# Broadcast rows, V copies and inverse deviations moved to other engines in a fused adaLN, sliding-window attention and token-mixer kernel

## The chip, the core and the metric

The kernel runs on one core of a Trainium2 chip. The core has five engines with instruction streams of their own: TensorE (PE, matrix products, with its weight loads listed as PEld), VectorE (DVE), ScalarE (ACT), GpSimd (POOL) and SyncE (SP, which here only issues DMAs). The metric is the device time of one execution in microseconds (us).

## The reference

One sequence of 2048 tokens (`S`), width 512 (`D`), 32 heads of 16. All inputs are bf16.

```python
mod = (silu(c) @ w_mod).reshape(1, 6, 1, 512)          # c: (1, 512), w_mod: (512, 3072)
sa, ca, ga, sb, cb, gb = mod[:, 0], ..., mod[:, 5]

h = layernorm(x) * (1 + ca) + sa
q, k, v = split(h @ wqkv)                              # 32 heads of 16
p = softmax(mask(q @ k.T * 16**-0.5))                  # key j for query i: 0 <= i - j < 256
x = x + ga * ((p @ v) @ wo)

h = layernorm(x) * (1 + cb) + sb
n = layernorm(h)
u = gelu(n.T @ w1 + b1)                                # over tokens: w1 is (2048, 1792)
y = (u @ w2 + b2).T                                    # w2 is (1792, 2048)
x = x + gb * y
```

## The kernel before

**Groups and chunks.** Tokens are worked on in four groups `G` of 512 (four tiles of 128 rows). Each group has a normalisation (`l1st` statistics, `l1rs` the inverse deviation, `l1nm` the negated mean, `xn` the normalised tile), transposes (`tr`), the modulation while the transposes are evicted (`h1T`), the products `q`, `k`, `v`, then attention, and then `post`: the output product (`wo`), the residual (`x2`), two more normalisations (`l2`, `l3`) and the modulation `c2`, `s2` between them, which give `hb`. Attention runs in eight units `u` of 256 queries, cut into 75 chunks. Chunk `i` is a score product `S{i}` into four PSUM banks (tiles `psa`, three banks, one buffer, and `psb`, one bank, two buffers), two exponentials on ACT (`E{i}` over three banks, `F{i}` over the fourth, both into `et`), for chunks 35 to 74 masks on DVE (`M{i}`; the earlier chunks add the mask inside PE), and the product `AV{i}` with V and with ones into `pxy`. When a unit's four heads' block is done, ACT takes `ln` and `rz` (tile `lz`, the reciprocal of the sum) and DVE multiplies (`OT`).

After attention come the products of the token mixer. `p` and `p2` are the parts over token groups that are ready early (tile `pu`, added up in `part`), `m1` the rest, `m2m` the second layer; `f1`, `f2` finish the output tiles.

**Order.** Nothing is scheduled at run time. Every piece of work is an `op` with a number, and the string `ORDER` (lines 45 to 99) lists all 1388 of them; `run_order` emits them in that order, and a letter behind a number (A, D, P) sets the engine where there is a choice of ACT, DVE or POOL. So each engine has a fixed instruction order, and an engine whose next instruction has to wait holds up everything behind it. All instructions from `ORDER` show in the profile under line L194, that of the wrapper which emits them, so they are told apart by tile names.

**PSUM.** Almost all products other than scores share two banks, `psd`, in turn (tiles `pq`, `pv`, `pt`, `pa`, `pu`, `ps_b`). PE can start the next of them when the one two earlier has been evicted.

**What the change touches.**

- *First shift.* For the first 256 tokens Q and K are made from `h1p`, which has the scale `1 + ca` alone, and the shift `sa` reaches them as a bias `qkb` from a product of `wqkv` with `sa2` (`e_b`, `e_bc2`, op `qkb`). V uses `h1T`, with scale and shift. Both kernels have this.
- *Modulation rows* `ga`, `1+cb`, `sb`, `gb`, wanted in all 128 partitions: `bc` makes the four rows in one PSUM bank, each in its own 32 partitions (four products at a time in different columns of the array, weights `sT_rep` of 32 columns), `bce` evicts them with a factor and an addend per partition, `bcw` writes 4 KB to a DRAM scratch and `bcl` reads that back to all partitions as `bc_all`.
- *Inverse deviation* (`e_rs`): on ACT as Ln and then Exp (x -0.5), or on POOL as an addition and a power. `ORDER` sends the nine of groups 1 to 3 (first norm) and 0 to 2 (second and third norm) to POOL.
- *V* (`v(tb)`, 16 tiles of tokens): the product leaves PSUM in a layout of two halves, one for each parity of heads, and each parity goes to its own 64 partitions of `VT`, with zeros in the other 64. For group 0 two copies `ve` of 64 partitions (8 in all) write into a `VT` that was zeroed before (`vz`). For groups 1 to 3 one copy `vn` of 128 partitions goes to SBUF, and two POOL multiplications `vp` by 1 or 0 (`half_m`) write both halves of `VT`, data and zeros.

Of the kernel before, what the change touches and what calls it, by code (L numbers as in the profile page):

```python
# [45 lines left out]
43 3 0 4 41 2 36 1 48 7 52 8 40 5 87 56 34 80P 6 46 9 57 37 10 58 84 39 11 33 12 88 35 13 50 14 59 89 31 90D 15 60  # L46
16 54 61 51 95D 17 65 96D 18 63 66 19 104 20 64 99 108A 47 21 67 53 100A 22 68 91 102A 23 24 105A 118 55 25 45 107A
101D 26 92 106A 119 27 115 103A 42 28 121 32 116 83P 120 49 62 69 117D 141 70 142 81D 133 143A 134 323 146 135A 147
38 136 148A 130 324 131 145 44 132A 149 137 150 325 138 151A 139 93 194 94D 140A 326 126 97P 195 122 144 123 82P 127
196 198 128D 327P 129A 98D 199 124D 153 71 125D 152 328D 200 109 72 73 206 110A 111D 207 112 74 197 114D 113D 201  # L50
180 181 202 154 182D 155 203 214 184 208 204 161 85 29 156D 215 162 788 30 205 209 164D 177 210 178 216 163D 222 211
165 223 212 183 166 179D 157 168D 158 167A 213 159D 217 224 160D 188 218 76 229 79 219 172 230 189 220 173 77 221
225 190D 174D 191 169 226 548 170 231 176 233 175 227 171D 185 234 186 192 228 193 329D 232 330D 331D 237 235 332D
333 187D 238 334 337 336D 338 236 335D 339D 245 239 340D 344 246 549 354 345 78 249 247 346D 355 250 348 240 356D
364 365 241 256 366D 251 388 257 789 349 389 242 260 258 243 350 261 244 351D 248 252 390D 264 253 550 391 262 372
265 75 358 373 86 369 374D 370 254 272 371D 266 341 273 551 380 381 255 342 382D 274 276 343D 384 259 277 263 347
359 267 357 278 394 360 395 352 286 361D 375 287 268 288 398 367 396 283 790 399 376 284 385 285 552P 386 269 402
400 270 791 363 271 403 275 368 279 387D 295 280 362 411 404 377 281 353 289 412 282 378 392 397 379D 393 553P 415
413 554P 296 401 416 383 405 290 555D 292 406 556D 422 417 291 557P 293 407 423 558 408 410 559 294 409 414 560D 424
427 297 418 428 561D 562 563 605 565D 419 431 564D 429 298 606 432 584 300D 299P 585 607D 420 586D 439 433 613 421  # L60
440 594 301D 595 302P 444 441 426 425 303D 792P 445 614 430 615D 451 446 596D 617 434 452 569 304P 570 443 435 305D
455 1033 453 571D 306P 1032 597 456 602 598 616 436 460 307P 457 437 603 313 461 308P 438 442 599D 447 604D 462 468
309P 448 589 469 590 579 310P 591D 449 472 588 470 450 580 314 473 459 454 572 458 311D 593 581D 480 474 566 793D
481 609 567 608 463 568D 464 484 315 601 482 574 485 592 610 575 600 465 488 486 582 466 576D 489 467 471 587 475
583 476 497 477 573 611 490 478 618 1031 612D 498 483 487 794D 312D 491 795P 316 492 501 499 508 479 796P 502 509
511 317P 512 493 619 503 494 797P 318D 620 495 510 500 320P 504 520 321P 505 625 513 621 517 506 319D 624 514 626
322P 507 515 622 496 577 521 630 627 578 518 516 631 519 623 628 639 632 522 798 640 802 799 803 523 633 644 641
524P 629 645 804D 634 525D 800D 526P 635 801D 652 646 805D 806 653 642 807 527D 809 808D 810 528P 636 657 654 811D
814 658 637 819 529D 815 647 530D 662 659 816D 638 663 643 660 648 531D 538 842 649 671 664 655 843 650 532D 672 820
651 533P 656 821D 665 676 673 661 677 534P 844D 853 539 666 667 535P 684 678 540 854 685 850 818 855D 851 536D 837  # L70
668 852D 537P 686 689 669 838 690 834 839D 835 674 694 691 679 670 687 695 675 692 680 836D 829 681 541 703 696 845
682 846 542P 704 683 830 697 688 543D 708 705 831D 546P 693 709 824 547D 812 698 847D 825 699 544D 716 710 545P 826D
1038 717 1039 706 1043 822 1040 700 721 711 718 1041 857 701 722 1044 1042D 840 702 707 813 726 723 1049 856 727 712
841 1045 713 735 832 728 1046 736 1050 827 1047D 1048 1051 858 1035 724 1052 714 817 740 1053D 737 751 741 719 752
848 715 748 720 729 742 859 823 725 753 860 730 743 1054 849 749 731 864 861 833 750 1055 865 1056 760 828 1060 1061
738 732 869 866 733 1057 761 870 734 1059 739 1058D 1034 744 1037 871 878 1062 745 872 879 1065 1066 867 1063 746
883 1064D 880 1067 747 884 1068 881 757 1070 1069D 758 1036 862 891 885 759 754 892 755 863 756 868 893 762 873 896
874 1071 897 763 1072 1073 894 764P 1076 886 875 898 901 876 1074 765D 902 766P 1077 1075D 877 767D 910 903 899 882
911 768D 887 769D 1078 770D 1082 888 771D 912 778 915 1083 916 1084 904 1085 1079 772D 889 917 923 1081 890 924 895
918 1080D 900 905 773D 913 906 928 1087 907 925 1088 908 774D 929 909 926 914 775P 779 919 920 933 776D 930 1086D  # L80
1089 777P 934 1090 780 1093 1094 1091D 921 942 781 935 987 943 1095 922 782P 1096 936 927 944 931 947 988 948 1097D
932 783D 989 937 786P 990 938 999 949 785P 955 991 939 787P 956 1098 992 1099 784P 940 1100 1001 1101 1000 957 960
1103 1102D 1115 961 950 1116 1007 1118 945 1119 1002 1008 965 1117 962 941 946 966 1009 951 1120 1121 963 952 1104
1010 967 974 1011 953 1105 968 975 1122 1106 958 1107 954 1123 976 979 959 980 977 964 1108D 969 1124 1012 970 1109
1019 971 1125 981 972 1110 1020 982 973 1126 978 983 1021 993 984 1157 1171 1027 1111 985 1166 1112 1022 1092 986
1163 994 1028 1113A 1158 995 996 1159 997 1170 1003 1161 1127 1162 1128 998 1160 1004 1176 1114 1129 1130 1165 1131
1013 1167 1005 1133 1164 1188 1169 1014 1180 1006 1168 1132 1134 1015 1136 1135 1137 1016 1172 1138 1139 1200 1017
1023 1140 1184 1018 1142 1024 1025 1143 1141 1026 1029 1145 1030 1146 1144 1173 1177 1174 1189 1192 1175 1178 1204
1147 1179 1181 1185 1182 1201 1205 1186 1148 1187 1190 1193 1149 1183 1208 1191 1212 1194 1209 1150 1195 1196 1197
1151 1198 1152 1220 1199 1153 1221 1202 1154 1216 1203 1206 1155 1213 1156 1248 1210 1238 1239 1214 1258 1224 1215  # L90
1240 1207 1217 1228 1211 1218 1229 1259 1222 1241 1268 1230 1225 1260 1226 1231 1249 1227 1232 1223 1242 1278 1219
1298 1261 1233 1243 1288 1262 1250 1279 1251 1299 1252 1289 1253 1300 1254 1280 1234 1244 1235 1301 1281 1245 1282
1290 1255 1263 1246 1318 1308 1236 1283 1269 1237 1284 1270 1309 1291 1319 1310 1292 1311 1302 1271 1320 1321 1272
1264 1328 1265 1303 1273 1256 1274 1322 1275 1338 1312 1285 1329 1266 1348 1293 1267 1323 1257 1349 1247 1330 1331
1332 1324 1294 1339 1276 1340 1358 1295 1277 1333 1304 1296 1313 1286 1297 1359 1360 1305 1287 1314 1361 1315 1368
1350 1325 1334 1362 1316 1351 1326 1363 1341 1306 1342 1352 1335 1307 1369 1317 1343 1327 1344 1370 1345 1353 1378
1336 1354 1346 1371 1379 1355 1347 1364 1337 1372 1356 1373 1365 1357 1374 1380 1375 1381 1382 1376 1383 1366 1384
1385 1367 1377 1386 1387
# [55 lines left out]
def kernel(  # L154
# [62 lines left out]
    half_t = const.tile([P, 4], F32, name="half_t")  # L217
    nc.vector.memset(half_t[:], -0.5)
    ident_v = identity[:].rearrange("p (a two d) -> p a two d", two=2, d=DH)
    half_m = const.tile([P, 2], F32, name="half_m")  # L220
    nc.vector.memset(half_m[:], 0.0)
    nc.vector.memset(half_m[0:KB, 0:1], 1.0)
    nc.vector.memset(half_m[KB:P, 1:2], 1.0)
    mask_par = const.tile([P, 2], F32, name="mask_par")
    modFM = const.tile([P, 8], F32, name="modFM")
    bc_all = const.tile([P, ND * D], BF, name="bc_all")
    bc_ga, bc_cb1, bc_sb, bc_gb = (bc_all[:, n * D : (n + 1) * D] for n in range(ND))
    b1FM = const.tile([P, NF], F32, name="b1FM")
    b2FM = const.tile([P, NT], F32, name="b2FM")
    wod = const.tile([P, ND, D], BF, name="wod")  # L230

    maskt = const.tile([P, 4, KB], BF, name="maskt")
# [158 lines left out]
    bcs = modw.tile([P, D], BF, name="bcs")  # L391
    bc_m = const.tile([P, 2], F32, name="bc_m")
    nc.vector.memset(bc_m[:, 0:1], 1.0)
    nc.vector.memset(bc_m[:, 1:2], 0.0)
    nc.vector.memset(bc_m[0:32, 0:1], ZSCALE)
    nc.vector.memset(bc_m[32:64, 1:2], 1.0)

# [865 lines left out]
```

## Time and profile before

| | |
|---|---|
| median of 3 runs | 266.56 us (266.38 to 267.31) |
| the profiled execution, its own time | 266.56 us |
| its span in the profile | 264.8 us |
| PE busy | 248.2 us (94%) |
| DVE busy | 193.5 us (73%) |
| ACT busy | 185.4 us (70%) |
| POOL busy | 95.9 us (36%) |
| DMA | 25.35 MB, mean 96 GB/s |
| granted PE clock | 1.00 throughout |

Times in the profile count from the start of the span. A busy share is taken over the whole span, and the kernel has stages with different limits: loading and the first chunks, attention from the first `E0` at 17.38 us to the last `F74` at 185.9 us, and a tail of matrix products after it. Rows of a timeline give the start, the duration and the number of instructions; durations of neighbours on ACT and DVE overlap a little, so the distance from start to start (the pitch) is what one instruction takes from its engine.

### The profile page before, as it was taken

Reading aid. Unit: us, or ns where it says so; the run is one execution under the profiler, and the core shown is the slowest. Engines: PE = TensorE matmul, PEld = TensorE weight load, DVE = VectorE, ACT = ScalarE, POOL = GpSimd, SP = SyncE. Lnnn points to the kernel's source line nnn. Section 1 sums busy time; section 2 is a strip of 40 time slices with the busy share of each in tenths; the row PEclk is TensorE's granted clock in tenths of the full one; section 3 lists DMA queues with packets and bytes.
Section 4 is the critical chain, followed back from the end, with each engine's and each line's share of the span. In section 5 each row is a group of like instructions: output and inputs, shape, how many; then the busy total and the mean of one; then the engine's idle time right before and its main releaser. Section 6 shows DMA issues by size and latency. Waiting matters only on the chain.

```text
span 264.8 us, 10695 instructions
## 1 busy us (share of the span) xinstructions
PE 248.2 (94%) x4769; PEld 136.8 (52%) x4769; DVE 193.5 (73%) x435; ACT 185.4 (70%) x268; POOL 95.9 (36%) x182
## 2 busy tenths in 40 slices
PE   7898999999998988899999999999999999999993
PEld 2576667656556654455544454445444444444441
DVE  5778896777847359999948888999998730415875
ACT  3479999999999899999999999999416431000000
POOL 8755321495289945553893031440000000000000
PEclk9999999999999999999999999999999999999999
DMA  7995400000017000000014862020499800001122
GB/s 212 369 382 197 42 5 6 2 5 2 2 49 196 5 4 5 2 2 2 5 38 128 227 172 85 2 61 23 152 362 397 360 2 0 21 0 63 59 99 79
DMA packets 31599, 25.35 MB, mean 96 GB/s; under 512 B 6076, under 2 KB 29632, under 8 KB 31552
## 3 DMA queue, kind: packets, MB, share of 16 engines
q1 hardware_dynamic: 31544, 24.66, 29.5%
q8 instruction: 37, 0.61, 0.9%
q14 instruction: 10, 0.08, 0.1%
q10 hardware_dynamic: 8, 0.00, 0.0%
HBM read 22.55 MB, written 2.10 MB: 93 GB/s over the span
## 4 chain that ended last, share of the span: by engine, by line
PE 67%; ACT 19%; DVE 8%; issue 4%; POOL 0%; ACTq 0%; POOLq 0%
PE pu L194 32%; ACT et L194 15%; PE pxy L194 13%; PE psa L194 8%; PE pq L194 5%; PE pa L194 4%; PE pv L194 3%; ACT lz L194 3%; DVE st L194 2%; DVE VT L194 1%; PE pt L194 1%; DVE part L194 1%; DVE OT L194 1%; PE psb L194 1%; DVE h L194 1%
## 5 line engine op out<-in xcount | busy, mean ns | idle before, releaser
L194 ACT ACTIVATE et<-psa 128x1536 bf16<-128x1536 f32 x75 | 109.1, 1455 | 4.0 <-PE psa L194 2.1
L194 PE MATMUL pu<-hb,w1p 128*128 128x512 bf16 x224 | 53.1, 380 | 0.8 <-DVE part L194 0.8
L194 PE MATMUL pu<-guT,w 128*128 128x512 bf16 x224 | 49.0, 379 | 0.0
L194 ACT ACTIVATE et<-psb 128x512 bf16<-128x512 f32 x75 | 45.1, 601 | 0.0
L194 PE MATMUL pxy<-et,ones_bd 128*32 128x192 bf16 (+3 forms) x960 | 38.7, 233 | 0.9 <-issue 0.9
L194 PE MATMUL pxy<-et,VT 128*32 128x192 bf16 (+3 forms) x960 | 38.4, 234 | 0.9 <-DVE OT L194 0.5
L194 PEld LDWEIGHTS <-w 128*128 128x128 bf16 x224 | 21.9, 98 | 26.4
L194 PE MATMUL psa<-QT,KT 32*128 32x192 bf16 (+3 forms) x720 | 29.8, 230 | 5.6 <-ACT et L194 4.9
L194 PEld LDWEIGHTS <-w1p 128*128 128x128 bf16 x224 | 20.3, 98 | 25.5 <-issue 2.3
L194 POOL TENSOR_SCALAR KT<-kb,mask_par 128x512 bf16<-128x512 bf16 (+1 forms) x36 | 22.9, 645 | 25.9 <-DVE kb L194 22.2
L194 PE MATMUL pq<-h1T,wqkv 128*128 128x512 bf16 (+1 forms) x128 | 30.1, 355 | 0.3 <-ACT VT L194 0.3
L194 PEld LDWEIGHTS <-KT 32*128 32x128 bf16 x960 | 16.1, 92 | 26.2 <-issue 23.9
L194 PEld LDWEIGHTS <-VT 128*32 128x32 bf16 x960 | 23.6, 96 | 11.6 <-issue 10.1
L194 PE MATMUL psb<-QT,KT 32*128 32x192 bf16 (+3 forms) x240 | 29.3, 231 | 0.0
L194 DVE SCALAR_TENSOR_TENSOR o<-pu,b2FM,bc_all 128x512 f32<-128x512 f32 x16 | 11.6, 748 | 20.2 <-PE pu L194 20.0
L194 DVE TENSOR_TENSOR et<-et,maskt 128x512 bf16<-128x512 bf16 (+2 forms) x56 | 24.9, 480 | 0.6 <-ACT et L194 0.5
L194 PEld LDWEIGHTS <-ones_bd 128*32 128x32 bf16 x960 | 23.2, 97 | 1.2 <-issue 1.1
L194 DVE BATCH_NORM_STATS2 st<-x 128x6 f32<-128x512 bf16 x32 | 21.7, 680 | 1.3 <-DMA x<-in_A_x_dram 1.1
L194 DVE TENSOR_TENSOR OT<-pxy,lz 128x256 bf16<-128x256 f32 x32 | 13.4, 420 | 10.6 <-ACT lz L194 10.1
L194 PEld LDWEIGHTS <-wqkv 128*128 128x128 bf16 x192 | 14.0, 97 | 13.4 <-issue 4.8
L194 PE MATMUL pv<-wqkv,h1T 128*32 128x256 bf16 x512 | 17.9, 274 | 0.2 <-DVE VT L194 0.2
L194 PE MATMUL pa<-wod,OT 128*128 128x512 bf16 x64 | 17.3, 381 | 0.3 <-ACT part L194 0.3
(113 smaller groups left out, 358.2 us busy)
## 6 DMA issues: line engine op xcount, KB each, us to landing
w1p<-in_B_w_dram SPq DMA_DIRECT2D x14, 512.0 KB, 6.1
w<-in_B_w_dram SPq DMA_DIRECT2D x14, 512.0 KB, 8.4
wmod<-in_w_mod_dram SPq DMA_DIRECT2D x6, 512.0 KB, 5.5
x<-in_A_x_dram SPq DMA_DIRECT2D x16, 128.0 KB, 4.8
out_dram<-otile SPq DMA_DIRECT2D x16, 128.0 KB, 1.7
wqkv<-in_A_wqkv_dram SPq DMA_DIRECT2D x2, 384.0 KB, 5.4
wqkv<-in_A_wqkv_dram SPq DMA_DIRECT2D x1, 512.0 KB, 5.0
wod<-in_A_wo_dram SPq DMA_DIRECT2D x1, 512.0 KB, 8.4
```

The costliest lines, as they stand in the source:

```text
L194: ins = call(*args, **kwargs)
```

## The change

It replaces four things and the order.

1. The four modulation rows are made as full products: `sT_rep` gets 128 columns, and each of `bc2`, `bc5`, `bc4`, `bc3` is four matrix products of 128x128 by 512 in a `psd` bank of its own, evicted by DVE (`bce`) into its own tile. The scratch, the two DMAs, `bc_m` and its four memsets go.
2. `e_rs` has ACT's form alone; the nine POOL ones become Ln and Exp on ACT.
3. All 16 tiles of V leave PSUM as two copies `ve` of 64 partitions; `vn`, `vp`, `half_m` and its memsets go, and all three `VT` buffers are zeroed (12 `vz` in place of 4).
4. `ORDER` is a new list. Read off it, in each engine's order:
   - SP: the same loads in the same order up to `x15`; then `b1`, `b2` without `bcw`, `bcl`.
   - PE: `S0` stands directly behind the Q and K products of heads' block 0 (before: behind those of all four blocks); `S1` behind Q and K of blocks 1 and 3 and one V tile (before: two V tiles); `S2` behind those of block 2 and the second V tile. `bc2` stands between `S7` and `S8`, `bc5` between `S8` and `S9`, `bc4` between `S15` and `S16`, `bc3` between `S17` and `S18` (before: `bc` between `S1` and `S2`).
   - ACT: one `h1p` in place of four, one `ke` in place of three, two `qe` in place of three; the others go to DVE. The nine added Ln and Exp pairs stand after `E5`, `E18`, `E19`, `F24`, `E32`, `E38`, `E47`, `E61` (behind `rz`) and `E68` (behind `rz`).
   - DVE: 30 `ve` in place of 6 and 12 `vn`, 4 `bce` in place of 1, `n2` 13 (9), `hb` 9 (7), `s2` 11 (10), `xn` 6 (10), `vz` 3 (1), negated means 4 (10).
   - POOL: without 24 `vp` and 9 inverse deviations; `vz` 9 (3), `xn` 10 (6), `n2` 3 (7), `hb` 7 (9), negated means 7 (1).

```diff
-    bc_all = const.tile([P, ND * D], BF, name="bc_all")
-    bc_ga, bc_cb1, bc_sb, bc_gb = (bc_all[:, n * D : (n + 1) * D] for n in range(ND))
+    bc_ga = const.tile([P, D], BF, name="bc_ga")
...
-    sT_rep = modw.tile([P, ND, 32], BF, name="sT_rep")
+    sT_rep = modw.tile([P, ND, P], BF, name="sT_rep")
...
-    def e_bc(e):
-        box["bc"] = ps_d.tile([P, D], F32, name="ps_b", tag="psd")
-        for k in range(ND):
-            for n, (v, _) in enumerate(bc_of):
+    for n, (v, dst) in enumerate(((2, bc_ga), (4, bc_cb1), (3, bc_sb), (5, bc_gb))):
+        def e_bc(e, v=v):
+            box["bc", v] = ps_d.tile([P, D], F32, name="ps_b", tag="psd")
+            for k in range(ND):
                 te.matmul(
-                    box["bc"][32 * n : 32 * n + 32, :], lhsT=sT_rep[:, k, :], rhs=wmod[:, k, v * D : (v + 1) * D],
-                    start=(k == 0), stop=(k == ND - 1), tile_position=(0, 32 * n),
+                    box["bc", v][:], lhsT=sT_rep[:, k, :], rhs=wmod[:, k, v * D : (v + 1) * D],
+                    start=(k == 0), stop=(k == ND - 1),
                 )
...
-    c0 = op("bcw", {"SP": 0.64}, lambda e: sp.dma_start(out=scratch[:], in_=bcs[0:P:32, :]), deps=[b], pos=9.5, nbytes=4 * KBT)
-    mod_ops.append(op("bcl", {"SP": 0.64}, lambda e: sp.dma_start(
-        out=bc_all[:], in_=scratch[:].rearrange("n d -> (n d)").unsqueeze(0).to_broadcast([P, ND * D])), deps=[c0], pos=9.5, nbytes=512 * KBT))
+            if v == 2:
+                ve.tensor_scalar(
+                    out=dst[:], in0=box["bc", v][:], scalar1=ZSCALE, scalar2=0.0, op0=ALU.mult, op1=ALU.add,
+                )
+            elif v == 4:
+                ve.tensor_scalar_add(out=dst[:], in0=box["bc", v][:], scalar1=1.0)
+            else:
+                ve.tensor_copy(out=dst[:], in_=box["bc", v][:])
...
         def e_rs(e, a, b):
             mv, rs, _ = box[box_key]
-            if e == "POOL":
-                po.tensor_scalar(out=rs[:, a:b], in0=mv[:, a:b, 1], scalar1=EPS, scalar2=0.0, op0=ALU.add, op1=ALU.add)
-                po.tensor_tensor(out=rs[:, a:b], in0=rs[:, a:b], in1=half_t[:, a:b], op=ALU.pow)
-                return
             ac.activation(out=rs[:, a:b], in_=mv[:, a:b, 1], func=ACT.Ln, bias=eps_t[:], scale=1.0)
             ac.activation(out=rs[:, a:b], in_=rs[:, a:b], func=ACT.Exp, scale=-0.5)
...
-            if G:
-                war = [av_ops[2 * G - 4, g] for g in range(ND)] if G >= 3 else []
-                vn = op("vn", {"ACT": 0.495, "DVE": 0.6}, e_vn, deps=[halves[1]] + vn_last.get(tb % 4, []), pos=pos)
-                halves[0].frees = [vn]
-                bs = [op("vp", {"POOL": 0.78}, lambda e, par=par: e_vp(e, par), deps=[vn, o_mp] + war, pos=pos, sh=True) for par in range(2)]
-                vn_last[tb % 4] = bs
-            else:
-                bs = [op("ve", {"ACT": 0.53, "DVE": 0.62}, lambda e, par=par: e_ve(e, par), deps=[halves[1], vt_zero[0][tb]], pos=pos)
-                      for par in range(2)]
-                halves[0].frees = bs
+            war = [av_ops[2 * G - 4, g] for g in range(ND)] if G >= 3 else [vt_zero[r3][tb]]
+            bs = [op("ve", {"ACT": 0.53, "DVE": 0.62}, lambda e, par=par: e_ve(e, par), deps=[halves[1]] + war, pos=pos)
+                  for par in range(2)]
+            halves[0].frees = bs
```

## The prediction

> **What bounds the kernel now.** I read the busy times by stage first, then groups with shapes kept apart, then ACT's timeline. By stage (columns: length; busy time and instructions of PE, PEld, DVE, ACT, POOL; PE clock; DMA share; GB/s):
>
> ```profile
> 0.00:17.40 17.40, 14.96 (x169) 8.57 (x173) 12.80 (x50) 8.06 (x20) 11.90 (x55) 1.00 0.95 313
> 17.40:40.00 22.60, 20.47 (x604) 14.59 (x600) 18.41 (x45) 20.99 (x30) 9.47 (x26) 1.00 0.43 113
> 40.00:80.00 40.00, 38.90 (x1183) 24.46 (x1174) 27.70 (x59) 38.42 (x52) 22.13 (x35) 1.00 0.06 16
> 80.00:130.00 50.00, 44.86 (x1335) 28.38 (x1334) 40.53 (x94) 48.81 (x65) 32.09 (x43) 1.00 0.10 26
> 130.00:186.00 56.00, 55.44 (x1100) 27.46 (x1099) 47.38 (x111) 54.55 (x77) 20.29 (x26) 1.00 0.33 87
> 186.00:199.10 13.10, 12.08 (x114) 5.68 (x113) 12.42 (x29) 4.05 (x15) 0.00 (x0) 1.00 0.78 275
> 199.10:264.80 65.70, 61.46 (x284) 27.69 (x283) 34.26 (x53) 10.51 (x15) 0.00 (x0) 1.00 0.28 106
> ```
>
> From 17.4 to 186 us ACT is busy 162.8 of 168.6 us and PE 159.7. Two engines set the pace by turns: ACT from 80 to 130 (48.8 of 50), PE from 130 to 186 (55.4 of 56), both from 40 to 80. DVE has room on average (134.0 of 168.6), but none in one stretch; ten microseconds each:
>
> ```profile
> 100.00:110.00 10.00, 7.82 (x159) 4.33 (x158) 9.84 (x25) 9.98 (x13) 5.70 (x9) 1.00 0.01 2
> 110.00:120.00 10.00, 9.47 (x269) 5.67 (x268) 9.66 (x24) 9.99 (x15) 5.42 (x5) 1.00 0.01 3
> 120.00:130.00 10.00, 9.73 (x273) 5.88 (x271) 9.36 (x23) 9.99 (x14) 4.88 (x7) 1.00 0.02 5
> ```
>
> POOL is nowhere the bound. The tail from 199.1 us is 284 matrix products on PE, 61.47 us, 0.2165 us each, and the change leaves it alone. So the change takes work from the engine with room (POOL) and gives it to the three that have little. The groups with the prices:
>
> ```profile
> L194 POOL TENSOR_SCALAR VT<-vn,half_m 128x512 bf16<-128x512 bf16 x24 | 17.3, 728 | 0.0
> L194 POOL TENSOR_TENSOR rs<-rs,half_t 128x4 f32<-128x4 f32 x9 | 9.9, 1104 | 0.8
> L194 DVE CAST vn<-pv 128x512 bf16<-128x512 f32 x12 | 8.3, 688 | 5.0 <-PE pv L194 4.9
> L194 DVE CAST VT<-pv 64x512 bf16<-64x512 f32 x6 | 4.1, 688 | 2.0 <-PE pv L194 1.9
> L194 PE MATMUL ps_b<-wmod,sT_rep 128*32 128x512 bf16 x16 | 1.0, 381 | 1.0 <-ACT VT L194 1.0
> ```
>
> A copy of 64 partitions costs DVE as much as one of 128 (688 ns both). Last, ACT's timeline with a chunk without `lz`, and one in which Ln and Exp of an inverse deviation stand:
>
> ```profile
> 51.39 1.45 ACT L194 ACTIVATE et<-psa 128x1536 bf16<-128x1536 f32 x1 [0.34 <-PE psb L194]
> 52.74 0.59 ACT L194 ACTIVATE et<-psb 128x512 bf16<-128x512 f32 x1
> 53.49 1.45 ACT L194 ACTIVATE et<-psa 128x1536 bf16<-128x1536 f32 x1 [0.16 <-PE psb L194]
> ...
> 173.98 1.46 ACT L194 ACTIVATE et<-psa 128x1536 bf16<-128x1536 f32 x1
> 175.31 0.31 ACT L194 ACTIVATE rs<-mv,eps_t 128x1 f32<-128x1 f32 x1
> 175.65 0.20 ACT L194 ACTIVATE rs<-rs 128x1 f32<-128x1 f32 x1
> 175.76 0.58 ACT L194 ACTIVATE et<-psb 128x512 bf16<-128x512 f32 x1
> ```
>
> Start to start, `E` takes 1.35 us and `F` 0.48; the pair Ln and Exp takes 0.45 (175.31 to 175.76). A chunk without `lz` still lasts 2.1 us (51.39 to 53.49), because the next scores wait for `E` to empty `psa`: some 0.25 us of ACT is free in it.
>
> **Part 1, Ln and Exp back on ACT.** Nine pairs at 0.45 us are 4.05 us, the upper bound; nothing is the lower. Six stand in chunks without `lz`, where 0.25 is covered and 0.2 remains, three beside `rz`, at the full 0.45: 6 x 0.2 + 3 x 0.45 = 2.55. Those of chunks 18, 19, 61 and 68 fall where PE limits as well; I take **+2.0 us**. Each pair waits for DVE's statistics, and behind it on ACT queue the next `E` and `F`; today these waits lie on POOL (32.3 us in six waits), where they cost nothing. By the page "ScalarE: Activation LUTs" of the Trainium skill (What ACT_TABLE_LOAD costs: 280 ns with a pointer bias, 186 without, about 93 of overlap each) a pair would be an estimated 0.29 us and nine 2.6. The row's 0.45 decides: its Exp has to wait for its Ln.
>
> **Part 2, the modulation rows.** 16 products of 128 columns at 0.2165 us are 3.46 us on PE; the 16 they replace take 1.05 (20.44 to 21.49). PE gets **2.4 us** more, in chunks 7 to 18, and the old ones' 0.96 us wait ahead of them at 20.44 goes. DVE gets three evictions more at 0.6 us (1.8). The two DMAs on SP go: `bc_all` lands 5.1 us after its issue at 24.29, by 29.4, and its first reader starts at 30.56 without a wait, so this gains nothing; `b1` and `b2` behind them on SP are read much later.
>
> **Part 3, V.** DVE gets 24 copies for 12, at a pitch of 0.6 us: 7.2 us. POOL loses 17.3 + 12.9 us and gets six `vz` at 0.95. Each V tile holds its `psd` bank for two copies, 1.2 us, where one did; PE's next product but one waits behind it. With bookkeeping moved between DVE and POOL by the new order (`n2` +4, `hb` +2, `s2` +1 and `xn` -4 at 0.33, `vz` +2 at 0.48, three evictions and three `h1p` from ACT at 0.35, negated means -6 at 0.13) DVE gets some 12 us, and in 17.4 to 186 us stands at about 145 of 168.6. From 80 to 130 it gets 8 copies (4.8) and about 1 us of `n2` and `hb`: 46.3 of 50, where the last three fifths hold 28.9 of 30 already today. Between nothing (all fits into 80 to 100 and behind 130) and 5.8 us (all of it stalls) I take **+1.5**, nearer the first, as 80 to 100 has 8 us free.
>
> One rule of the skill speaks for this part of the change: "SBUF — State Buffer" (Who interferes with whom) says that a DVE instruction with two SBUF inputs and a GpSimd one that reads SBUF block each other for a whole instruction. If each of the 24 `vp` held DVE up for its length, DVE would win back an estimated 17 us, and the change would gain. The trace shows much less. Three of DVE's mask products at 130.31 us, beside `vp` and `kk`, take 1.67 us together, two at 109.00 take 0.75; but all 32 of that shape average 461 ns, where one alone at 111.89 takes 420, so the excess is about 32 x 0.04 = 1.3 us, and it is POOL that stretches (`vp` 679 to 1383 ns). I count this relief as part of the spread.
>
> **Part 4, the first chunks.** `S0` runs at 16.63 us today behind 32 products that only later chunks need part of. In the new order it needs block 0 alone: `kd` ends at 12.4 today. ACT's queue puts a pair (`l1rs`) and a `ke` ahead of `E0`, which should start at about 14.4. Between `S0` and `S1` PE no longer has 8 K and Q products (1.0 us, 15.59 to 16.63) and one V tile (1.0): `S1` moves from 18.96 to about 17.0 and `E1` from 20.41, where ACT waited for a V copy, to about 17.5. `S2` follows 1.0 + 1.0 us of PE work later, and without `bc` and its wait: `E2` at about 19.8 instead of 22.68, `E3` 22.1 instead of 25.26. A lead of **3.2 us**, between nothing (the DVE queue, which now has `h1p` and `ke`, delays `S0` and the banks) and 4.
>
> Most of it is borrowed: what PE skipped comes later. By `S8` PE owes `AV5`, `AV6`, two transposes (1.2 us) and three of the four modulation products (2.6): 3.8 us, while PE idles only 1.1 us from 40 to 80 to pay it. So **+2.7 us** come back before chunk 27; this contains part 2's 2.4.
>
> **Sum.** -3.2 + 2.7 + 2.0 + 1.5 = +3.0 us. The last norm chain (186 to 199) and the tail keep their work. The profiled execution took 266.56 us, its span 264.8 and 1.76 around it, and equals the median of the runs: 269.6 us.
>
> **The rivals.** *DVE becomes the bound of chunks 26 to 50* (slower too): the 5.8 us of 80 to 130 do not fit in front, ACT waits for statistics and PE for banks. Then 5.8 stand for 1.5, and Part 1 is whole at 2.5: 274.4. For it: three stretches at 9.4 to 9.8. Against: DVE idle before and after. *The lead is kept* (faster): PE work that I count as paid back slips into the 6.2 us that PE idles from 80 to 130 and 186 to 199, and the pairs on ACT take half of what I give them: -3.2 + 1.0 + 0.0 = -2.2, 264.4. It decides if `E27` starts over 2 us sooner than its 80 us of today. For it: ACT alone limits from 80 to 130, so a lead that ACT has there stays. Against: PE is full from 40 to 80. *Nothing to see*: lead and costs cancel, within 1.3 us.
>
> **How the numbers follow.** About 0.5% (1.3 us) is what a measurement of this kernel can tell from no change. Forecast 0.55, DVE-bound 0.15, lead kept 0.16, cancelled 0.14. Slower is the first two, 0.70; same 0.14; faster 0.16. The forecast's own spread is 267.9 to 272.5. The range reaches to the middle of the DVE case and near that of the lead: 264.8 to 274.4.
>
> **What would show it.** Right: `E0` at about 14.4 and `E3` near 22; `E27` within 1 us of 80; ACT busy up by about 4 us in 17.4 to 186, DVE by 10 to 12; POOL down by 24; the last `F74` at about 189 instead of 185.9; a tail of 61.5 us behind it. Wrong: `F74` before 186 (the lead is kept), PE waiting for DVE's V copies by several us or ACT for DVE's statistics inside attention (DVE bounds), or no lead at `E3`.

## The result, and the profile after

The changed kernel takes 270.26 us (270.12 to 271.32) beside 266.51 us for the kernel before on the same chip: a ratio of 1.0143, 95% interval 1.011 to 1.0176, so 3.75 us more. The profiled execution took 270.39 us, its span is 268.7.

First the page, busy time and the chain that ended last:

```profile
PE 251.1 (93%) x4769; PEld 137.3 (51%) x4769; DVE 208.0 (77%) x447; ACT 186.5 (69%) x280; POOL 69.4 (26%) x149
...
PE 65%; DVE 21%; ACT 8%; issue 2%; DMA 2%; SPq 1%; DVEq 0%
```

The chain of before, for comparison:

```profile
PE 67%; ACT 19%; DVE 8%; issue 4%; POOL 0%; ACTq 0%; POOLq 0%
```

DVE has 14.5 us more work than before and POOL 26.5 less. In the chain ACT and DVE have changed places, and PE is about where it was. By stage, cut at the same times as before (same columns):

```profile
0.00:17.40 17.40, 15.86 (x205) 9.02 (x206) 13.28 (x43) 9.09 (x18) 13.61 (x57) 1.00 0.95 299
17.40:40.00 22.60, 20.66 (x601) 14.98 (x603) 19.53 (x45) 20.11 (x29) 13.73 (x31) 1.00 0.39 100
40.00:80.00 40.00, 38.48 (x1177) 24.45 (x1180) 31.42 (x66) 38.13 (x55) 10.28 (x17) 1.00 0.02 4
80.00:130.00 50.00, 43.59 (x1203) 26.12 (x1192) 46.41 (x101) 48.10 (x69) 23.75 (x34) 1.00 0.30 77
130.00:186.00 56.00, 55.48 (x1167) 27.95 (x1169) 47.37 (x109) 53.74 (x78) 8.02 (x11) 1.00 0.22 59
186.00:199.10 13.10, 12.35 (x154) 5.72 (x143) 12.26 (x30) 5.75 (x16) 0.00 (x0) 1.00 0.69 239
199.10:268.70 69.60, 64.73 (x299) 29.05 (x297) 37.73 (x62) 11.62 (x19) 0.00 (x0) 1.00 0.26 99
```

From 80 to 130 us DVE is busy 46.41 of 50, and both PE (43.59 for 44.86) and ACT (48.10 for 48.81) do less than before: they wait. Where the time goes is read best from the starts of the `E` exponentials in ACT's timeline, one per chunk. The rows of `E0`, before and after:

```profile
17.38 1.44 ACT L194 ACTIVATE et<-psa 128x1536 bf16<-128x1536 f32 x1
...
14.11 1.44 ACT L194 ACTIVATE et<-psa 128x1536 bf16<-128x1536 f32 x1
```

All of them read in this way:

| chunk | before, us | after, us | difference, us |
|---|---|---|---|
| E0 | 17.38 | 14.11 | -3.27 |
| E2 | 22.68 | 21.27 | -1.41 |
| E3 | 25.26 | 23.34 | -1.92 |
| E7 | 36.18 | 32.98 | -3.20 |
| E8 | 38.28 | 35.67 | -2.61 |
| E16 | 55.59 | 54.63 | -0.96 |
| E27 | 79.88 | 79.29 | -0.59 |
| E42 | 113.05 | 113.01 | -0.04 |
| E50 | 130.11 | 131.91 | +1.80 |
| E54 | 138.48 | 140.89 | +2.41 |
| E70 | 173.98 | 176.33 | +2.35 |
| E74 | 183.23 | 186.76 | +3.53 |

The attention begins 3.3 us sooner, has given that back by chunk 42, loses 2.4 us from chunk 42 to 54, and 1.2 more at the end. The products of the tail take 0.2165 us each as before; in the chain there are 280 of them after and 284 before (before, then after):

```profile
199.14 61.47 PE pu L194 x284
...
203.51 60.61 PE pu L194 x280
```

The stretch of chunks 42 to 54 in that chain (start, duration, engine and tile; before, `ACT et` and PE had most of it):

```profile
111.72 1.76 DVE et L194 x2
113.48 0.60 DVE QT L194
114.09 0.61 DVE st L194
114.72 0.18 DVE mv L194
114.90 0.57 DVE VT L194
115.48 0.70 DVE VT L194
116.19 0.68 DVE VT L194
116.88 0.33 DVE et L194
117.21 0.03 issue
117.24 0.69 DVE VT L194
```

Here DVE is the bound: masks, Q evictions, statistics and V copies one behind the other, with nothing between them but 0.03 us of issue. The four `VT` lines are the copies of two V tiles; two `vn` did this before. The group of them:

```profile
L194 DVE CAST VT<-pv 64x512 bf16<-64x512 f32 x30 | 20.6, 686 | 2.9 <-PE pv L194 1.3 <-ACT VT L194 1.0
```

At the start, ACT's timeline shows why `E2` leads by 1.4 us only. A V copy stands ahead of it on ACT and waits 1.82 us, first for PE's product and then for DVE's copy of the other parity:

```profile
18.37 0.58 ACT L194 ACTIVATE et<-psb 128x512 bf16<-128x512 f32 x1
20.78 0.59 ACT L194 ACTIVATE VT<-pv 64x512 bf16<-64x512 f32 x1 [1.82 <-DVE VT L194]
21.27 1.43 ACT L194 ACTIVATE et<-psa 128x1536 bf16<-128x1536 f32 x1
```

### The profile page after: what moved, and what is told of

Its sections match the earlier page's. It is cut to its first block, busy times and chain, and to the rows that moved or that the text cites. A ratio compares the mean times of both kernels' runs of the same rounds, so it can differ in the third digit from the quotient of the medians.

```text
span 268.7 us, 10681 instructions
## 1 busy us (share of the span) xinstructions
PE 251.1 (93%) x4769; PEld 137.3 (51%) x4769; DVE 208.0 (77%) x447; ACT 186.5 (69%) x280; POOL 69.4 (26%) x149
## 4 chain that ended last, share of the span: by engine, by line
PE 65%; DVE 21%; ACT 8%; issue 2%; DMA 2%; SPq 1%; DVEq 0%
PE pu L194 32%; PE pxy L194 10%; PE psa L194 7%; PE pq L194 7%; ACT et L194 6%; DVE VT L194 4%; DVE st L194 3%; PE pv L194 3%; PE pa L194 3%; DVE et L194 3%; DMA x<-in_A_x_dram 2%; DVE part L194 2%; DVE kb L194 1%; DVE h1T L194 1%; DVE h L194 1%
## 5 line engine op out<-in xcount | busy, mean ns | idle before, releaser
L194 PE MATMUL pu<-hb,w1p 128*128 128x512 bf16 x224 | 53.9, 380 | 1.1 <-DVE part L194 0.9
L194 PE MATMUL pq<-h1T,wqkv 128*128 128x512 bf16 (+1 forms) x128 | 29.4, 354 | 1.1 <-DVE VT L194 0.8
L194 DVE SCALAR_TENSOR_TENSOR o<-pu,b2FM,bc_gb 128x512 f32<-128x512 f32 x16 | 11.9, 749 | 22.8 <-PE pu L194 22.6
L194 PEld LDWEIGHTS <-KT 32*128 32x128 bf16 x960 | 14.9, 92 | 27.0 <-issue 24.8
L194 DVE TENSOR_TENSOR et<-et,maskt 128x512 bf16<-128x512 bf16 (+2 forms) x56 | 25.9, 493 | 0.8 <-ACT et L194 0.8
L194 DVE CAST VT<-pv 64x512 bf16<-64x512 f32 x30 | 20.6, 686 | 2.9 <-PE pv L194 1.3
```

What stands on the lines that cost most here:

```text
L194: ins = call(*args, **kwargs)
```

## The experiments

My theory was the sum of the prediction: a lead of the first chunks, paid back by PE, plus a price for the pairs on ACT and one for V. The rival: the parts lie in waits that are there anyway, and the order itself costs the time. Every ratio below is to the kernel before, run beside it on the same chip.

**One part undone, in the new order.** Each of these takes the changed kernel and gives one part back its old form; the operations that come back stand in the new list where their inputs are ready.

*Inverse deviations on POOL again* (`x1_rs_on_pool`); the nine operations carry the letter P:

```diff
+            if e == "POOL":
+                po.tensor_scalar(out=rs[:, a:b], in0=mv[:, a:b, 1], scalar1=EPS, scalar2=0.0, op0=ALU.add, op1=ALU.add)
+                po.tensor_tensor(out=rs[:, a:b], in0=rs[:, a:b], in1=half_t[:, a:b], op=ALU.pow)
+                return
```

> The changed kernel with one part undone: the nine inverse deviations of groups 0 to 3 run on POOL again (addition and power), at the same places of the order. Theory of the prediction (part 1 is worth 2.0 us): about 268.3 us against 270.3 of the changed kernel, E39 to E50 some 1 to 1.5 us earlier, ACT busy down by 4 us. Rival 1, ACT limits everywhere: the whole 4 us come back, 266.3. Rival 2, DVE is the bound of the middle chunks: ACT's pairs only filled waits, 270 within 0.5.

*One product of four row blocks, with the DRAM scratch* (`x2_one_bc`), ahead of `S4`:

```diff
-    for n, (v, dst) in enumerate(((2, bc_ga), (4, bc_cb1), (3, bc_sb), (5, bc_gb))):
-        def e_bc(e, v=v):
+    def e_bc(e):
...
+    c0 = op("bcw", {"SP": 0.64}, lambda e: sp.dma_start(out=scratch[:], in_=bcs[0:P:32, :]), deps=[b], pos=9.5, nbytes=4 * KBT)
```

> The changed kernel with the modulation rows made as before: one bank with four products in different columns at a time, placed ahead of S4, scratch and broadcast read back by DMA. Theory (PE from S8 to S18 is full, 2.4 us of PE work are paid whole there): the lead over the kernel before stays near 2.5 us at E16 instead of 1.0; at the end 268.5 to 269 us, some of it lost again to DVE in chunks 43 to 52. Rival, the four products lie in PE's waits: 270 within 0.5 and the lead at E16 still 1.0.

*V by one copy and two POOL multiplications* (`x3_v_by_pool`) for groups 1 to 3:

```diff
+            if G:
+                war = [av_ops[2 * G - 4, g] for g in range(ND)] if G >= 3 else []
+                vn = op("vn", {"ACT": 0.495, "DVE": 0.6}, e_vn, deps=[halves[1]] + vn_last.get(tb % 4, []), pos=pos)
+                halves[0].frees = [vn]
+                bs = [op("vp", {"POOL": 0.78}, lambda e, par=par: e_vp(e, par), deps=[vn, o_mp] + war, pos=pos, sh=True) for par in range(2)]
```

> The changed kernel with V of groups 1 to 3 going out as one DVE copy and two POOL multiplications again, the POOL pair listed directly behind the copy. Theory (the loss of 2.2 us from E39 to E52 is DVE's, which the second V copy overfills): that stretch keeps the pace of the kernel before, 268 to 268.8 us. Rival 1, that loss comes from ACT's pairs: it stays, 270 within 0.5. Rival 2, a V tile that waits for POOL stops PE: slower than 270.3.

*All three undone, only the new order left* (`x4_order_alone`), the three edits together:

> All three parts undone and only the new order kept (with one row product ahead of S4, V and inverse deviations by POOL at the new order's places). Theory (the order gives a lead of about 3 us in the first chunks that the three parts use up): the lead stays, 264 to 265.5 us, below the kernel before. Rival, the lead is borrowed whatever the parts, since PE is full from 40 to 80: 266.5 within 0.7, the time of the kernel before.

| | time, us | ratio (95%) | E8, us against before | E42 | E74 |
|---|---|---|---|---|---|
| changed kernel | 270.26 | 1.0143 (1.011 to 1.0176) | -2.61 | -0.04 | +3.53 |
| x1 | 272.15 | 1.0197 (1.0176 to 1.0219) | -1.55 | +1.97 | +5.52 |
| x2 | 272.02 | 1.021 (1.0174 to 1.0245) | +0.14 | +2.34 | +6.11 |
| x3 | 275.03 | 1.0308 (1.0284 to 1.0331) | -1.43 | +1.05 | +8.09 |
| x4 | 278.89 | 1.0438 (1.0414 to 1.0462) | -0.33 | +6.07 | +12.68 |

None is faster than the changed kernel, and x3 and x4 are slower well beyond the intervals; each against its own comparison run, the four are 1.1 to 8.0 us worse, where a part with a price should have given time back. The trace of x3 shows why such a run prices the wrong thing. Its `vp` group stands in POOL's fixed queue ahead of an `xn` for which DVE waits (timeline, POOL and DVE, then PE):

```profile
116.68 2.86 POOL L194 TENSOR_SCALAR VT<-vn,half_m 128x512 bf16<-128x512 bf16 x4 [1.01 <-DVE vn L194]
...
119.54 0.76 POOL L194 TENSOR_SCALAR xn<-x,nm,rs 128x512 bf16<-128x512 bf16 x1
...
120.33 0.91 DVE L194 TENSOR_TENSOR h<-xn,bc_cb 128x512 bf16<-128x512 bf16 x1 [2.69 <-POOL xn L194]
...
123.26 0.41 DVE L194 TENSOR_TENSOR OT<-pxy,lz 128x256 bf16<-128x256 f32 x1
...
123.72 0.41 PE L194 MATMUL pxy<-et,VT 128*32 128x256 bf16 x4 [3.04 <-DVE OT L194]
```

Four `vp` hold `xn`; `xn` holds DVE's `h` for 2.69 us; behind `h` on DVE stands `OT`, and PE waits 3.04 us for that. This one knot is worth 3.1 us from `E44` to `E46`. It is paid twice, as the clock in the windows after it shows (columns as above):

```profile
117.00:120.00 3.00, 2.42 (x42) 1.13 (x34) 0.64 (x2) 3.00 (x4) 3.00 (x5) 1.00 0.02 5
120.00:123.00 3.00, 0.40 (x8) 0.21 (x8) 2.67 (x5) 2.85 (x5) 2.25 (x3) 0.91 0.00 0
123.00:126.00 3.00, 2.28 (x52) 1.80 (x51) 2.97 (x9) 0.00 (x0) 0.00 (x0) 0.50 0.00 0
126.00:129.00 3.00, 3.00 (x60) 1.18 (x52) 2.93 (x8) 1.87 (x3) 0.03 (x1) 0.50 0.00 0
129.00:132.00 3.00, 2.57 (x90) 1.70 (x90) 2.40 (x6) 2.97 (x7) 1.22 (x3) 0.95 0.03 8
```

The granted clock falls to 0.50 within PE's 3.04 us of idling and stays there for some six microseconds after it, and `E48` is another 1.4 us late, where the changed kernel loses 0.5. So these runs refute no price of a part and confirm none: the new list was laid out for the parts that it has, and a part put back can find its queue taken. The trace of x3 shows this; for x1 and x2 it is argued.

**Parts left out in place.** The second set keeps the changed kernel and every place in its order, and leaves the work of a part out.

*Without the nine added Ln and Exp pairs* (`y1_no_pairs`):

```diff
+            if b - a == 4:
+                return
             ac.activation(out=rs[:, a:b], in_=mv[:, a:b, 1], func=ACT.Ln, bias=eps_t[:], scale=1.0)
```

> The changed kernel and its order, with the nine Ln and Exp pairs of groups of four tiles left out (those inverse deviations are a constant 1, written once at the start). Nothing else moves, so this shows what the pairs cost in place. Theory (part 1 at 2.0 us): 268.3 against 270.3 of the changed kernel. Rival, ACT limits everywhere: 266.2 (the whole 4.05 us). Rival, they lie in waits: 270 within 0.5.

*A quarter of the modulation products* (`y2_bc_quarter`):

```diff
-            for k in range(ND):
+            for k in range(1):
```

> The changed kernel and its order, with only the first of the four products of each modulation row (three quarters of the sum left out): 2.6 us less on PE, all DVE evictions kept. Theory (PE full from S8 to S18): the loss of the lead from E8 to E16 (1.65 us) all but goes, and the end is 1 to 2 us earlier, 268.3 to 269.3. Rival, PE has that room and the end is set later: 270 within 0.5.

*One V copy instead of two for groups 1 to 3* (`y3_one_copy`):

```diff
+                if G and par:
+                    return
```

> The changed kernel and its order, with one of the two V copies of each tile of groups 1 to 3 left out: 12 copies or 7.2 us less on DVE, and the PSUM bank held for one copy, as before the change, but without POOL's part. Theory (part 3 at 1.5 us; in the trace after, E39 to E52 lose 2.2 us): 268 to 268.8. Rival, DVE is the bound of the middle chunks: 5 us or more, below 265.5. Rival, that loss is ACT's: 270 within 0.5.

*All three left out* (`y4_all_left_out`):

> The three together left out of the changed kernel: its order with the work of before the change or less on PE, ACT and DVE. Theory (the order's early start is worth about 3 us, and the three parts use up more than that): 264 to 265 us, with the lead of E5 kept to the end. Rival, the early start is borrowed from PE in any case: 266 to 267.

| | time, us | ratio (95%) | E0, us against before | E26 | E42 | E54 | E74 |
|---|---|---|---|---|---|---|---|
| changed kernel | 270.26 | 1.0143 (1.011 to 1.0176) | -3.27 | -0.59 | -0.04 | +2.41 | +3.53 |
| y1 | 270.85 | 1.0142 (1.012 to 1.0164) | -2.47 | +0.12 | +0.84 | +3.29 | +3.99 |
| y2 | 272.07 | 1.0176 (1.0148 to 1.0203) | -2.29 | -0.01 | +1.98 | +4.44 | +5.24 |
| y3 | 269.11 | 1.0079 (1.0058 to 1.0101) | -2.37 | -0.16 | +0.10 | +1.31 | +2.65 |
| y4 | 269.61 | 1.0095 (1.0072 to 1.0118) | -2.82 | -0.92 | +0.30 | +1.52 | +2.47 |

`E0` differs by up to 1 us between these profiles although nothing ahead of it is changed, so I compare what a run gains or loses after it. The pairs: from `E0` to `E74` y1 loses 6.46 us where the changed kernel loses 6.80, so nine pairs are worth 0.3 us here; the ratios of y1 and of the changed kernel are equal. The products: from `E0` to `E26` y2 loses 2.28 and the changed kernel 2.68, so three quarters of the products (2.6 us of PE work) are worth 0.4; then y2 loses 1.3 us between `E26` and `E28`, which the changed kernel doesn't, and gains nothing in all. PE's timeline shows that loss (y2, then y4): in the middle of the scores of chunk 28 PE stands idle for nothing that the trace shows, which the view calls "issue".

```profile
83.14 0.20 PE L194 MATMUL psa<-edge_t,edge_w 32*128 32x64 bf16 x2 [1.24 <-issue]
...
81.61 0.20 PE L194 MATMUL psa<-edge_t,edge_w 32*128 32x64 bf16 x2 [0.63 <-issue]
```

The changed kernel, y1 and y3 have no such idling there. Why the two runs without the products have it stays open; it is no price of the products or of the order.

The second V copies: y3 loses 5.02, 1.8 less, and the ratios say 0.64%, 1.7 us. From `E42` to `E54` it loses 1.21 for 2.45: half of that stretch is V. Each of these comparisons of two ratios is uncertain by about 1 us, as the intervals say.

With all three left out, y4 is still 0.95% over the kernel before, 2.5 us. So about 1.3 of the 3.75 us is the work of the three parts. Of the 2.5, y4 loses 0.7 between `E26` and `E28`, with the idling of PE above, which the changed kernel doesn't have. Taken off, **1.8 to 2.5 us remain with the order** and 1.3 to 2.0 with the parts, which fits the 2.1 to 2.5 of the three runs added up. The order here takes in what it moves between the engines, and three evictions of modulation rows and eight `vz` that y4 keeps.

In y4 DVE has hardly more to do in the middle chunks than before: windows of ten microseconds from 97 to 137 give it 34.40 us of 40, before 33.93. Yet y4 loses 1.22 us from `E42` to `E54`, in this window (before, then y4):

```profile
117.00:127.00 10.00, 9.63 (x232) 5.23 (x235) 9.37 (x22) 9.99 (x14) 5.21 (x6) 1.00 0.01 2
117.00:127.00 10.00, 7.97 (x220) 4.91 (x223) 9.63 (x25) 9.64 (x15) 2.92 (x4) 1.00 0.01 3
```

PE is busy 7.97 us there for 9.63 before, DVE 9.63 for 9.37. From 112 to 142 us DVE has some 22% of y4's chain and none of that of before. DVE's work is nearly the same and its sequence is not, so the sequence is the likely cause; which of the moved operations does it wasn't singled out.

**Parts put singly into the kernel before.** The third set starts from the other end: the kernel before and its order, with one part of the change.

*The first chunks in the new order, up to `S2`* (`z1_ramp_alone`), only `ORDER` edited:

> The kernel before, all its parts, with only the first chunks in the new order: everything up to S2 stands as in the changed kernel, everything behind it as before (the two V copies of tile 0 directly behind S2). Theory, as it stands after the runs with parts left out: the early start is borrowed from PE, E0 at about 14.5 and E2 near 21.5, and the lead shrinks to under 1 us by E27: 266 to 267 us, the time of the kernel before. Rival, the lead is real where the modulation products are cheap: 264 to 265, faster than both kernels.

*V by two DVE copies* (`z2_v_dve`), with the twelve `vz`:

```diff
-                vn = op("vn", {"ACT": 0.495, "DVE": 0.6}, e_vn, deps=[halves[1]] + vn_last.get(tb % 4, []), pos=pos)
-                halves[0].frees = [vn]
...
+            war = [av_ops[2 * G - 4, g] for g in range(ND)] if G >= 3 else [vt_zero[r3][tb]]
+            bs = [op("ve", {"ACT": 0.53, "DVE": 0.62}, lambda e, par=par: e_ve(e, par), deps=[halves[1]] + war, pos=pos)
+                  for par in range(2)]
```

> The kernel before and its order, with V of groups 1 to 3 as two DVE copies at the place of the one, POOL's multiplications gone and eight more zeroings on POOL early. Theory (leaving out twelve copies gave back about 1.3 us): 267.5 to 269 us against 266.6. Rival, DVE takes them in its idle time: 266.6 within 0.5.

*The nine pairs on ACT* (`z3_pairs_on_act`), nine letters of `ORDER` from P to A:

> The kernel before and its order, with the nine inverse deviations as Ln and Exp on ACT instead of POOL. Leaving the pairs out of the changed kernel gave back nothing. Theory from that run: 266.6 within 0.5 as long as ACT does not wait for DVE's statistics. Prediction's part 1: 268.6. Rival, in this order the pairs stand where POOL's turn came, and ACT waits there for DVE: 270 or more.

*Four full modulation products* (`z4_four_bc`), the diff of the change's first point:

> The kernel before and its order, with the modulation rows as four full products (at the old place and behind S6, S8 and S10), each evicted by DVE, and no DMA. Prediction's step (2.4 us more on a full PE): 268 to 269. Theory from the run with a quarter of the products: PE takes them for 0.5 us or less, 266.6 to 267.3.

| | time, us | ratio (95%) | E0, us against before | E3 | E8 | E26 | E42 | E74 |
|---|---|---|---|---|---|---|---|---|
| z1 | 270.23 | 1.0096 (1.0068 to 1.0124) | -2.96 | +2.90 | +3.20 | +3.37 | +3.22 | +3.76 |
| z2 | 281.27 | 1.0509 (1.0476 to 1.0542) | +0.31 | +0.31 | +8.01 | +9.29 | +9.38 | +12.66 |
| z3 | 269.68 | 1.0084 (1.0058 to 1.0111) | -0.27 | -0.27 | -0.20 | +0.62 | +1.08 | +2.11 |
| z4 | 273.38 | 1.0223 (1.0193 to 1.0254) | +2.29 | +2.45 | +3.82 | +7.49 | +7.48 | +8.02 |

z3 is the clean one. It climbs in steps of up to 0.5 us and ends 2.24 us longer (269.68 less 267.44): in the old order, where ACT sets the pace, nine pairs cost about what I had put down, 2.0, and not the nothing that y1 had led me to expect.

z1 missed its question. The graft had to bring two tiles' statistics, the rows and a transposed block ahead of `E2`, so the lead is gone at `E2`, and at `E3` the run is 2.9 us behind: PE waits 2.29 us at 22.3 us for DVE's eviction of the rows (`bcs`), and its clock is 0.50 for some 3.4 us from 25.7 on. What it shows is the size of a debt of the start: 2.9 us at `E3` are 3.76 at `E74`. No slack swallows them. Whether the new order's first chunks would pay in the old kernel stays open.

z4 adds 5.0 us between `E6` and `E12`, where the prediction had 2.4 for the products and y2 0.4 for three quarters of them in the new order. Each inserted product is followed on PE by a wait for its own eviction:

```profile
36.27 1.04 PE L194 MATMUL ps_b<-wmod,sT_rep 128*128 128x512 bf16 x3
...
38.09 0.60 PE L194 MATMUL pq<-h1T,wqkv 128*128 128x256 bf16 x4 [0.78 <-DVE bc_gb L194]
```

It also starts 2.3 us late, behind a load of `wqkv` and a clock of 0.50 at 16 to 18 us; that part stands ahead of the first of the four products. The profiled execution (274.73 us) is the slowest of z4's six, of which the fastest took 272.61.

z2 loses 7.7 us at one place, between `E7` and `E8`, ahead of any added copy. Eight `vz` stand back to back on POOL there, and four DVE operations that took 1.37 us before take 8.46 (timeline; the first row is that of before):

```profile
34.46 1.37 DVE L194 TENSOR_SCALAR xn<-x,mv,rs 128x512 bf16<-128x512 bf16 x4
...
34.77 8.46 DVE L194 TENSOR_SCALAR xn<-x,mv,rs 128x512 bf16<-128x512 bf16 x4
...
34.93 7.19 POOL L194 MEMSET VT<- 128x1024 bf16 x8
...
42.33 1.89 PE L194 MATMUL pt<-identity,xn 128*128 128x128 bf16 x12 [5.88 <-DVE xn L194]
```

The first of the four takes 7.50 us of that, to the end of the last memset; the other three follow at their usual pace. PE waits 5.88 us, and its clock is 0.50 from 42 to 45. The V copies themselves are the rest: 1.3 us from `E8` to `E26` and 3.3 from `E42` to `E74`, nearly all of it by `E52`.

## Why the prediction held, step by step

**Sign and size.** +3.0 us were forecast and 3.75 came, 269.6 and 270.26 us. The named signs: `E0` at 14.4 (14.11), `E27` within 1 us of 80 (79.29), the last `F74` ending at about 189 (189.0), DVE at 46.3 of 50 from 80 to 130 (46.41) and up by 10 to 12 from 17.4 to 186 (10.7), POOL down by 24 (26.5). The tail's products take as long as they did. Several of the terms are right as sums and wrong in what they are made of.

That the sum came so near is in good part luck. Without the three parts it leaves -3.2 of lead and 0.3 of payback, so the order should have gained 2.9 us; y4 shows that it loses 1.8 to 2.5. The parts stand in the sum with 2.4 + 2.0 + 1.5 = 5.9 us, and in place they are worth 1.3 to 2.0. Two errors of some 4 to 5 us cancel.

**The lead** of 3.2 us is there at `E0` (3.27) and `E7` (3.20), though in the profiles of y1 to y4 `E0` leads by only 2.29 to 2.82. `E3` was to start at 22.1 and starts at 23.34: I had left out the wait of ACT's V copy. `E5` has the lead again, as ACT has room there.

**The payback** of 2.7 before chunk 27 measured 2.7 (-3.27 to -0.59). That it "contains part 2's 2.4" is wrong: y2 finds 0.4 for the products. y4 loses 1.9 of it without any of the three parts, so most is work that PE skipped at the start, or the order; without part 2 my sum left 0.3 for that.

**Part 1** failed by itself. I priced the pairs by chunks in which ACT alone limits, as it did before; put into the old order they cost 2.24 (z3), but in the changed kernel 0.3 (y1). From 17.4 to 186 us ACT waits 7.0 us there and 4.6 before, for PE but for 1.8 at the first V copies; with the pairs left out (y1) it waits 9.9, so most of their time had lain in those waits. ACT's busy time was to rise by 4 us in 17.4 to 186 and fell by 2.7.

**Part 3** was +1.5 and measured 1.7 to 1.8 (y3), to within about 1 us. The place is right too: DVE's queue is full from chunk 42 to 54. The rival in which DVE becomes the bound of chunks 26 to 50 is right in kind and wrong in size: DVE carries the chain, but the stretch costs 2.4 us, half of it V's, and not 5.8. Relief for DVE's masks from POOL's missing `vp`, which I had counted as spread, didn't come: 32 masks of 128x512 average 454 ns after 461, and the 16 of 128x256 went from 283 to 344.

**What the sum lacked** is a loss by the order itself, 1.8 to 2.5 us. The lead and the payback nearly cancel, the pairs are worth 0.3, and V alone wouldn't make 3.75; that 2.0 for the pairs and 2.4 for the products were too much hid that the order's own price was missing. The rivals on the other side fell: the lead isn't kept, as `E27` leads by 0.6 us and not by 2.

**Open:** which moves of the new order cost its 1.8 to 2.5 us. The 2.5 are what is left of a lead of 2.8 us at `E0` and of 5.3 lost behind it in y4: 1.9 to `E26` (some of it the skipped PE work), 1.1 to `E32` (0.7 of it PE's unexplained idling), 1.2 in chunks 42 to 54 with nearly the DVE work of before, 1.1 in the stretches between and the last chunks. The wait ahead of `E2` isn't among them, as `E5` has the lead again. None was tried alone; undoing them means laying out the list again.

## What to carry to other kernels

In a kernel whose order is written out, a part has no price of its own: the same nine pairs cost 2.24 us in one order and 0.3 in the other, and three parts that together are worth 1.3 to 2.0 us in place made the kernel slower by 8.0 us when their old forms were put into the new order. To price a part, leave its work out where it stands and change nothing else, and look in the trace for waits that only this run has (y2 lost 1.3 us to one); to forecast a change, sum the parts by the engine that sets the pace after the change, and give the order a term of its own. An engine that has room on average (DVE, 134 of 168.6 us) has to be read in stretches of ten microseconds before work is given to it.

## What the runs showed of the hardware

*POOL's memsets stop DVE.* Eight of 128x1024 in a row, 7.19 us, held one DVE operation for 7.50 us, where the three behind it took some 0.4 each (z2), though a memset reads nothing. "SBUF — State Buffer" (Who interferes with whom) of the Trainium skill says that some of DVE's one-input operations, `tensor_scalar` among them, can take a port pair that they share with GpSimd, and that whoever has it blocks the other for a whole instruction. The rows agree, and show more: the one DVE operation stood behind eight of POOL's instructions. The masks of the prediction have two inputs and are no measure of this. It is one instance; in the changed kernel no `xn` on DVE takes over 0.44 us, so it shows no such stall of them, and whether it matters that the memsets stand back to back was not tested.

*Waits of PE can halve its clock.* After waits of 3.04 us (x3) and 5.88 us (z2) the granted clock was 0.50 for about six and four microseconds. It fell to 0.50 after waits of 3.02 us (x4) and 2.29 (z1) too, and stayed at 1.00 after one of 2.03 (x4). z4 has it at 0.50 near 17 us with no wait of PE over 0.73 us in the ten before, so the length of one wait alone doesn't decide it. Read from windows of one microsecond, the whole stretch at 0.50 lasts about 3.4 us (x4, z1, z4) or 6.8 (x3, z2). In the changed kernel and the one before no wait of PE that the trace attributes is over 1.3 us, and both run at 1.00 throughout; a long wait inside attention can therefore be worth more than its length, in x3 3.1 us and then 0.9 beyond what the changed kernel loses there.
